# Value and column sums of a segment's attention in 32-row tiles of the PE array, with one half divided before its value sums

## The chip, the cores and the metric

One core of a Trainium2 chip runs the whole program. The metric is device time in microseconds for one execution. Engines are named as in the profile: PE (matmul), PEld (PE's weight loads), DVE (VectorE), ACT (ScalarE), POOL (GpSimd) and SP (which issues most DMAs).

## The reference, cut to what matters

Four blocks follow each other on a sequence of 2048 rows of 512: attention with a recurrent memory, a gMLP mixer, and both again. The attention works through 64 segments of 32 tokens. Each segment sees 8 memory rows ahead of its tokens, and the first 8 rows of its output are the next segment's memory, so that the segments form a chain.

```python
for s in range(n_seg):                                   # 64, one after the other
    h = jnp.concatenate([mem, xs], axis=1)               # 8 + 32 rows
    q, k, v = (einsum('btd,dhe->bhte', h, W) for W in (Wq, Wk, Wv))   # 32 heads of 128
    scores = jnp.where(mask, einsum('bhqe,bhke->bhqk', q, k) * scale, -1e9)
    o = einsum('bhqk,bhke->bhqe', softmax(scores), v)
    o = einsum('bhte,hed->btd', o, Wo)
    mem = o[:, :8, :]; outs.append(o[:, 8:, :])
```

## The kernel before

`a_block` holds one attention block, `b_block` one gMLP block. Inside `a_block`, `segment` is called 64 times. The order of the work on PE, DVE and ACT is the order in which the code records it (`manual_schedule`), and each of these engines takes its instructions strictly in that order. A recorded instruction that must wait holds up all behind it on its engine.

A segment has 40 positions: 8 memory rows, 24 tokens, and 8 last tokens whose rows do not depend on the memory of this segment as keys and are prepared a block of 128 rows ahead. `hT` holds the transposed input rows. `mm_chunk` (L710) projects 32 rows against 512 columns of weights: 16 matmuls in four column groups of 32 (tile 128*32), four K steps of 128. `qk` does so for Q (j = 0, 1) and K (j = 2, 3), each j being half r of the 32 heads; ACT casts the result to `rows`, and DVE turns 32x32 blocks (`qk_T`, L922) into `QQ` and `KA`. `v_mm` makes the values, cast into `VA`. `scores(r)` makes the scores of 16 heads; keys of the last 8 positions come from `KX`, and their values from `VX`. `exps` is ACT's exponential and `close` DVE's product with the mask.

In `close`, `maskN` writes E twice, with alternate groups of 32 rows set to zero, so that `sums_memory`, `pv` and `sums_tokens` (L971, L988, L991, L980) can work with 64-row tiles of the array (64*128 in the profile): two tiles at once, each summing over 64 rows of which 32 are zero. The column sums are divided by afterwards: Ln and Exp on ACT give the reciprocals `Rm` (memory positions) and `Rt` (all others), and DVE multiplies (`memory_out` L1007, `tok_out` L1010, `last_out` L1013). Each half r has its own psO tile of two PSUM banks (`attO0`, `attO1`); psQ and psS share the two-bank tile `att`.

`wo_pairs` (px) and `wo_rest` (pw) multiply the memory rows by Wo. `fold` adds the parts of px (`cross`, `t1`), and `build_hA` adds pw (`memT`, L893) and turns the sum into the next segment's `hT` (L894), which the next Q matmul needs. That is the recurrence.

Between these steps `fill()` takes one step of a generator: `b_units` projects the last 8 positions of the next 128 rows (psb), six chunks in three of every four segments (the fourth has no filler in the first four block rows); `y_part` multiplies finished rows by Wo (pwB). `copies`, `turns` and `adds` collect the casts and additions that follow, and `run` records them. `spare1`, `spare2`, `spare3` place statistics of rows (`x_stats`, `y_stats`) and additions (`y_half`) on DVE; `x_stats` and `y_stats` also append to `copies` a pair of ACT instructions that makes a reciprocal standard deviation (`_rstd_act`, RS in the profile) out of DVE's aggregate (MV).

## Time and profile before

| | |
|---|---|
| Median of 3 runs | 1644.34 us (1640.43 to 1645.09) |
| Span of the profiled execution | 1643.0 us |
| First Q matmul of the first segment | 30.4 us |
| Last Q of the first attention block's 64 segments starts | 687.6 us |
| First Q of the second attention block | 846.1 us |
| A segment, first Q matmul to first Q matmul | mostly 10.157 us; the very first 23.5 us |
| Granted TensorE clock, mean | 0.996 |

The profiled execution's own time is known by its span; the median of the runs is 1.3 us above it. The two gMLP blocks take what is between the attention blocks and at the end, some 145 us each. A line of the timeline gives start, duration, engine, source line, operation, what is written and read, the shape, and how many equal ones follow each other. A matmul's duration includes its drain through the array, which overlaps the matmuls after it; in `128*32` the first number is the tile's rows and the second its columns.

### The profile page before, as it was taken

The numbers are of one execution on the slowest core, as the hardware profiler recorded it, in microseconds if no ns is written. First come the engines' busy times: TensorE is split into PE (matmuls) and PEld (weight loads), VectorE is DVE, ScalarE is ACT, GpSimd is POOL, SyncE is SP. The second block draws the span as 40 slices with busy tenths as digits, with TensorE's granted clock in tenths as the row PEclk, the third lists the DMA queues.
The fourth block names the chain that finished last, engine by engine and source line by source line (L and its number), as shares of the span: only waits on it lengthen the run. The fifth ranks groups of instructions, "written<-read, shape, count | busy, mean of one in ns | idle before, by whom it ended". The sixth has DMA issues, their size and how long they took to land.

```text
span 1643.0 us, 87201 instructions
## 1 busy us (share of the span) xinstructions
PE 1593.0 (97%) x39134; PEld 945.6 (58%) x39134; DVE 1181.5 (72%) x2923; ACT 1072.8 (65%) x2281; POOL 288.1 (18%) x604
## 2 busy tenths in 40 slices
PE   5799999999999999999999999999999999999999
PEld 2455555555656566566655555556566565565565
DVE  3677777778877887884367777777788778878722
ACT  2677777777777777661047777777777777776400
POOL 5111111112211122320011111111122112214000
PEclk9999999999999999999999999999999999999999
DMA  9322121212321333277951222212233224335696
GB/s 362 86 42 42 42 45 42 43 43 75 80 55 43 77 86 80 87 190 143 210 167 46 47 46 46 48 44 45 59 89 86 46 58 95 89 71 155 152 198 159
DMA packets 263598, 148.78 MB, mean 91 GB/s; under 512 B 197560, under 2 KB 239648, under 8 KB 263224
## 3 DMA queue, kind: packets, MB, share of 16 engines
q1 hardware_dynamic: 249992, 99.38, 27.7%
q0 software_dynamic: 13232, 43.82, 8.3%
q8 instruction: 307, 5.03, 1.3%
q14 instruction: 67, 0.55, 0.1%
HBM read 59.68 MB, written 37.19 MB: 59 GB/s over the span
## 4 chain that ended last, share of the span: by engine, by line
PE 55%; DVE 1%; ACT 0%; issue 0%; DMA 0%; SPq 0%; DVEq 0%
PE pg L393 9%; PE psQ L710 7%; PE psK L710 7%; PE psb L710 5%; PE pz L292 5%; PE px L790 4%; PE psm L710 3%; PE psV L710 3%; PE psO L797 3%; PE py L436 2%; PE pwB L809 2%; PE psO L971 1%; PE psO L988 1%; PE psT L980 1%; PE psS L945 1%; PE pw L1237 0%
## 5 line engine op out<-in xcount | busy, mean ns | idle before, releaser
L710 PEld LDWEIGHTS <-hT 128*32 128x32 bf16 x12288 | 332.4, 97 | 309.0 <-DVE hT L894 28.5
L922 DVE STREAM_TRANSPOSE QQ<-rows 128x512 bf16<-128x512 bf16 x256 | 177.7, 694 | 57.6 <-ACT rows L919 57.0
L922 DVE STREAM_TRANSPOSE KA<-rows 128x512 bf16<-128x512 bf16 x256 | 176.1, 688 | 11.5 <-ACT rows L919 6.0
L1010 DVE TENSOR_TENSOR uT<-psO,Rt 128x384 bf16<-128x384 f32 x256 | 140.7, 550 | 36.1 <-ACT Rt L1078 35.7
L919 ACT CAST rows<-psQ 128x512 bf16<-128x512 f32 x256 | 142.4, 594 | 26.2 <-PE psQ L710 23.2
L393 PE MATMUL pg<-z,wspT 128*128 128x344 bf16 x1024 | 154.3, 309 | 0.0
L1078 ACT ACTIVATE Rt<-Rt 128x512 f32<-128x512 f32 x256 | 147.3, 622 | 4.1
L710 PE MATMUL psQ<-Wq_sb,hT 128*32 128x512 bf16 x2048 | 135.1, 382 | 13.1 <-DVE hT L894 9.0
L954 ACT ACTIVATE S<-psS 128x224 bf16<-128x224 f32 x256 | 91.4, 357 | 81.9 <-PE psS L949 81.9
L1007 DVE TENSOR_TENSOR uT<-psO,Rm 128x128 bf16<-128x128 f32 x256 | 74.6, 292 | 96.8 <-ACT Rm L1006 95.8
L880 POOL COPY KX<-old 128x128 bf16<-128x128 bf16 x128 | 69.4, 542 | 384.9 <-PE psS L949 244.5
L790 PEld LDWEIGHTS <-uT 128*32 128x32 bf16 x4608 | 110.8, 96 | 44.5 <-DVE uT L1007 32.2
L710 PE MATMUL psQ<-Wk_sb,hT 128*32 128x512 bf16 x2048 | 135.7, 383 | 0.0
L710 PE MATMUL psm<-Wq_sb,hT 128*32 128x512 bf16 x2048 | 135.0, 381 | 0.0
L790 PE MATMUL px<-Wo,uT 128*32 128x256 bf16 x3840 | 134.8, 274 | 0.0
L710 PE MATMUL psK<-Wk_sb,hT 128*32 128x512 bf16 x2048 | 133.9, 379 | 0.0
L710 PE MATMUL psK<-Wv_sb,hT 128*32 128x512 bf16 x2048 | 133.9, 379 | 0.0
L710 PE MATMUL psV<-Wv_sb,hT 128*32 128x512 bf16 x2048 | 133.2, 378 | 0.0
L1075 ACT ACTIVATE Rt<-psT 128x1024 f32<-128x1024 f32 x128 | 131.1, 1024 | 3.2
L880 POOL COPY KX<-front 128x128 bf16<-128x128 bf16 x126 | 67.9, 545 | 367.9 <-PE psS L949 247.3
L393 PEld LDWEIGHTS <-wspT 128*128 128x128 bf16 x1024 | 100.2, 98 | 53.2
L797 PE MATMUL psO<-Wo_high,uT 128*32 128x128 bf16 x7168 | 125.9, 219 | 2.5 <-issue 1.9
(195 smaller groups left out, 2864.9 us busy)
## 6 DMA issues: line engine op xcount, KB each, us to landing
o_d<-o_sb SPq DMA_DIRECT2D x126, 64.0 KB
vb_d<-front SPq DMA_DIRECT2D x30, 256.0 KB
VX<-vb_d SPq DMA_DIRECT2D x120, 64.0 KB
ln_x<-xd SPq DMA_DIRECT2D x26, 256.0 KB
y_o<-o_d POOLq DMA_DIRECT2D x22, 256.0 KB, 3.4
xd<-y_o POOLq DMA_DIRECT2D x22, 256.0 KB, 2.9
Wq_sb<-in_A_Wq_dram POOLq DMA_DIRECT2D x8, 512.0 KB, 8.8
Wk_sb<-in_A_Wk_dram POOLq DMA_DIRECT2D x8, 512.0 KB, 10.0
```

Of the source, the lines that this page charges most:

```text
L292: nc.tensor.matmul(pz[:, c0:c1], lhsT=xnT[:, kt, :], rhs=w_in_sb[:, kt, c0:c1], start=(kt == 0), stop=(kt == KT - 1))
L393: nc.tensor.matmul(pg[t][:, k, 0:344], lhsT=wsp[t][:, st, :], rhs=z(st, 344 * k, 344 * k + 344), start=(st == 0), stop=(st == NT - 1))
L710: return [nc.tensor.matmul(ps[32 * cg:32 * cg + 32, :], lhsT=lhs(kt, cg), rhs=rhs(kt, cg), start=(kt == 0), stop=(kt == KT - 1), tile_posi ...
L790: nc.tensor.matmul(px[at:at + 32, 0:256], lhsT=lhs[:, h, :], rhs=wo_rhs(h, slice(k + 2, None, -2) if h % 2 else slice(k, None, 2)), start= ...
L797: nc.tensor.matmul(pw[32 * cg:32 * cg + 32, :], lhsT=lhs[:, h, :], rhs=wo_rhs(h, cg), start=False, stop=(h == H - 1), tile_position=(0, 32 ...
L880: eng.tensor_copy(KX[:, :, r].rearrange("p g (k i) -> p i g k", i=4), bs["KTB"][:, r].rearrange("p (i g) k -> p i g k", i=4)[:, :, :, 8 * ...
L919: return r, mms, nc.scalar.copy(r[:], ps)
L922: nc.vector.transpose(out=QQ[:, j % 2, :, 0:32] if j < 2 else KA[:, j % 2], in_=r[:])
L954: return nc.scalar.activation(out=S[:, r], in_=psS[:, r, 0:224], func=ACT.Exp, scale=scale)
L1010: nc.vector.tensor_tensor(out=hview(uT_nxt[:], r, 0, 24), in0=oview(r, 8, 32), in1=rview(r, 0, 24), op=ALU.mult)
L1075: nc.scalar.activation(out=Rt[:], in_=psT[:], func=ACT.Ln)
L1078: nc.scalar.activation(out=rt, in_=rt, func=ACT.Exp, scale=-1.0)
```

## The change

- E is written once (`mask` in place of `maskN`), as one tile per half. `pv` and the column sums of the second half (`sums_one`) use tiles of 32 rows and 128 columns (32*128), four at a time, into one psO tile of four banks (`attO`) for both halves.
- The column sums of the first half (`sums_own`) are made before its value sums, with a matrix `group` of ones in each group of 32 rows, in tiles of 128*32. ACT makes their reciprocals `Rn`, and DVE divides E[0] by them ahead of `pv(0)`. Its results are then copied out of psO (`memory_zero`, a copy for the tokens on DVE, one for the last positions on ACT). The second half is divided afterwards as before (`memory_one`, `tokens_one`).
- `QQ` and `KA` keep two heads side by side, element by element. The casts write `rows` in that order, and DVE turns pairs of 16-bit elements as one 32-bit element (`bitcast(F32)`).
- The last key chunk (j = 3) is made, cast and turned in two halves, the first as PE's third item of the segment, in a bank of the psP tile (tag `attO`).
- V(0) and V(1) are spread over the scores and sums. Casts of j = 1, of the first half of j = 3 and of VA(0) are on DVE, that of VA(1) on ACT.
- Wo's fold: `memT` and its turn are made in two halves of 64 columns; pw has the tile `att1`.
- The fillers step by single K steps: two before the value sums, two after the sums, four at the end. ACT's order after Wo is: collected copies, copy for oB, Ln of Rt, cross, Exp of Rt.

The diff, cut to its core (lines that go are left out where new ones stand for them):

```diff
+    mask = cp.tile([P, 224], BF16, name="mask")
+    m4 = mask[:].rearrange("p (i c) -> p i c", i=4)
+    nc.vector.tensor_copy(m4[:, :, 0:40], maskf[:, 0:160].rearrange("p (i q) -> p i q", i=4))
+    nc.vector.tensor_copy(m4[:, :, 40:56], own)
+    group = cp.tile([P, 4, 32], BF16, name="group")
+    nc.vector.memset(group[:], 0.0)
+    for g in range(4):
+        nc.vector.memset(group[32 * g:32 * g + 32, g, :], 1.0)
...
+        att = [_Tagged(ps_pool, f"att{r}", 1) for r in range(2)]
+        attO = _Tagged(ps_pool, "attO", 1)
...
+        KAr = [pers.tile([P, 2, 8, 32, 2], BF16, name=f"KA{i}") for i in range(2)]
+        QQr = [pers.tile([P, 2, 8, 40, 2], BF16, name=f"QQ{i}") for i in range(NKQ)]
...
+                ps = (accB if early and k % 2 and not alone and not (now and j == 5) else accA).tile([P, 512], F32, name="psb")[:]
+                for kt in range(KT):
                     mm_chunk(ps, lambda kt, cg: bs["hB"][:, kt, :],
-                             lambda kt, cg: qk_rhs(w, j, kt, cg) if j < 4 and now else cols_rhs(w, j, kt, cg), kts)
-                    if kts[-1] != KT - 1:
+                             lambda kt, cg: qk_rhs(w, j, kt, cg) if j < 4 and now else cols_rhs(w, j, kt, cg), (kt,))
+                    if kt < KT - 1 and not early:
...
+                copies.append(out)
+                yield
...
+                                     start=(h == lo and h == WO_PAIR), stop=(h == H - 1), tile_position=(0, 32 * cg), skip_group_check=True)
...
+            eng.tensor_copy(QQ[:].rearrange("p r n q two -> p (r n) two q")[:, :, :, 32:40],
+                            bs["QTB"].rearrange("p r (n two) k -> p (r n) two k", two=2)[:, :, :, 8 * j4:8 * j4 + 8])
...
+            for k in range(2):
+                cols = slice(64 * k, 64 * k + 64)
+                nc.vector.tensor_tensor(out=t[:, cols], in0=pw[:, cols], in1=t1[:, cols], op=ALU.add)
+                nc.vector.transpose(out=rows.hT[s // 4][:, 2 * k:2 * k + 2, at:at + 32], in_=t[:, cols])
...
+            S = [segp.tile([P, 224], BF16, name=f"S{r}", bufs=1) for r in range(2)]
+            E = [segp.tile([P, 224], BF16, name=f"E{r}", bufs=1) for r in range(2)]
+            begin = first and s == 0
...
+            def qk_copy(eng, r, ps, h=0, n=1):
+                return eng(part(r, h, n).rearrange("p (n el two) -> p n two el", el=32, two=2), ps.rearrange("p (n two el) -> p n two el", el=32, two=2))
+
+            def qk_T(j, r, h=0, n=1):
+                t = QQ[:, j % 2, :, 0:32] if j < 2 else KA[:, j % 2, 8 * h // n:8 * (h + 1) // n]
+                nc.vector.transpose(out=t.bitcast(F32).rearrange("p n q one -> p n (q one)"), in_=part(r, h, n).bitcast(F32))
...
+                        nc.tensor.matmul(pS[32 * g:32 * g + 32, 56 * i:56 * i + 40], lhsT=KA[:, r, n // 2, :, n % 2], rhs=QQ[:, r, n // 2, :, n % 2],
+                                         start=(i == 0), stop=True, tile_position=(0, 32 * g), skip_group_check=True)
...
+                nc.scalar.activation(out=S[r][:], in_=psS[r][:, 0:224], func=ACT.Exp, scale=scale)
...
+            def sums_own(pN):
 
                 for k in range(2):
+                    for g in range(4):
+                        o, e = quad(pN[32 * g:32 * g + 32, :]), E[0][:]
+                        nc.tensor.matmul(two_ends(o) if k else o, lhsT=group[:, g, :],
+                                         rhs=e_own(e).rearrange("p i (b e) -> p i b e", b=2) if k else e_all(e, 0, 40),
+                                         start=False, stop=True, tile_position=(0, 32 * g), skip_group_check=True)
+
+            def sums_one(lo, at, n):
 
                 for k in range(2):
+                    for g in range(4):
+                        e = E[1][32 * g:32 * g + 32, :]
+                        o = quad(psO[:, g, at:at + 4 * n])
+                        b = 40 if lo == 0 else 48
+                        nc.tensor.matmul(o[:, :, n - 8:n] if k else o, lhsT=ones[32 * g:32 * g + 32, :],
+                                         rhs=e_all(e, b, b + 8) if k else e_all(e, lo, lo + n), start=False, stop=True,
+                                         tile_position=(32 * g, 0), skip_group_check=True)
...
+                        nc.tensor.matmul(psO[:, g, 160 * r + 40 * i:160 * r + 40 * i + 40], lhsT=VA[32 * g:32 * g + 32, r, i, :],
+                                         rhs=E[r][32 * g:32 * g + 32, 56 * i:56 * i + 40], start=(r == 0 and i == 0), stop=True,
+                                         tile_position=(32 * g, 0), skip_group_check=True)
+                for g in range(4):
+                    nc.tensor.matmul(two_ends(quad(psO[:, g, 160 * r:160 * r + 160])), lhsT=VX[32 * g:32 * g + 32, j4, r, :],
+                                     rhs=e_own(E[r][32 * g:32 * g + 32, :]).rearrange("p i (b e) -> p i b e", b=2), start=False, stop=True,
+                                     tile_position=(32 * g, 0), skip_group_check=True)
...
+            def memory_zero():
+                nc.vector.tensor_copy(hview(uT_cur[:], 0, 24, 32), oview(0, 0, 8))
+
+            def memory_one():
+                nc.vector.tensor_tensor(out=hview(uT_cur[:], 1, 24, 32), in0=oview(1, 0, 8), in1=Rm[:].rearrange("p g (i q) -> p g i q", q=8), op=ALU.mult)
...
+            psQ = att[0].tile([P, 512], F32, name="psQ")
+            qk(0, psQ)
+            psK = att[1].tile([P, 512], F32, name="psK")
+            qk(2, psK)
...
+            qk_copy(nc.scalar.copy, r0, psQ[:])
+            psP = attO.tile([P, 4, 512], F32, name="psP")
+            qk(3, psP[:, 0, 0:256], h=0, n=2)
             qk_T(0, r0)
+            r2 = new_rows()
+            qk_copy(nc.scalar.copy, r2, psK[:])
+            psM = accB.tile([P, 512], F32, name="psm")
+            qk(1, psM)
+            r3 = new_rows()
+            low = qk_copy(nc.vector.tensor_copy, r3, psP[:, 0, 0:256], 0, 2)
             qk_T(2, r2)
...
+            def values(kts):
+                mms = v_mm(0, psP[:, 1, :], kts)
+                other_bank(mms, [low] + high)
+                seen_v.extend(mms)
+
+            def last_keys():
+                mms = qk(3, psP[:, 2, 0:256], h=1, n=2)
+                other_bank(mms, [low])
+
...
+            values((0,))
+            psS[0] = att[0].tile([P, 512], F32, name="psS")
+            scores(0)
+            r1 = new_rows()
+            qk_copy(nc.vector.tensor_copy, r1, psM[:])
+            if not begin:
+                last_keys()
+            exps(0)
+            values((1,))
+            qk_T(3, r3, 0, 2)
+            close(0)
+            values((2,))
+            high.append(qk_copy(nc.scalar.copy, r3, psP[:, 2, 0:256], 1, 2))
+            other_bank(high, seen_v)
             qk_T(1, r1)
...
+            v_mm(1, psW, (0,))
+            pN = psS[0][:, 256:416]
+            sums_own(pN)
+            qk_T(3, r3, 1, 2)
+            values((3,))
+            v_mm(1, psW, (1,))
+            Rn = segp.tile([P, 160], F32, name="Rn", bufs=1)
+            nc.scalar.activation(out=Rn[:], in_=pN, func=ACT.Ln)
+            psS[1] = att[1].tile([P, 512], F32, name="psS1")
+            scores(1)
+            nc.vector.tensor_copy(VA[:, 0].rearrange("p i e -> p (i e)"), psP[:, 1, :])
+            v_mm(1, psW, (2, 3))
+            nc.scalar.activation(out=Rn[:], in_=Rn[:], func=ACT.Exp, scale=-1.0)
             exps(1)
...
+            e = E[0][:]
+            nc.vector.tensor_tensor(out=e_all(e, 0, 40), in0=e_all(e, 0, 40), in1=quad(Rn[:]), op=ALU.mult)
+            own = e_own(e).rearrange("p i (b e) -> p i b e", b=2)
+            nc.vector.tensor_tensor(out=own, in0=own, in1=two_ends(quad(Rn[:])), op=ALU.mult)
+            nc.scalar.copy(VA[:, 1].rearrange("p i e -> p (i e)"), psW[:])
             close(1)
...
+            spare1(E)
+            if not begin:
+                fill(2)
+
+            psO = attO.tile([P, 4, 512], F32, name="psO")
             pv(0)
...
+            sums_one(0, 320, 8)
             pv(1)
...
+            sums_one(8, 352, 32)
+            if not begin:
+                fill(2)
+            memory_zero()
+            Rm = segp.tile([P, 4, 32], F32, name="Rm", bufs=1)
+            nc.scalar.activation(out=Rm[:], in_=psO[:, :, 320:352], func=ACT.Ln)
+            nc.scalar.activation(out=Rm[:], in_=Rm[:], func=ACT.Exp, scale=-1.0)
+            memory_one()
...
             px = accB.tile([P, 512], F32, name="px")
             wo_pairs(px, uT_cur)
...
+            pw = att[1].tile([P, 512], F32, name="pw")[:, 0:128]
...
+            run(copies)
+            nc.scalar.copy(oB_cur[0], oview(0, 32, 40))
+            Rt = segp.tile([P, 4, 128], F32, name="Rt", tag="Rt", bufs=1)
+            nc.scalar.activation(out=Rt[:], in_=psO[:, :, 352:480], func=ACT.Ln)
+            run(turns)
+            spare2()
             cross = wk.tile([P, P], F32, name="cross", bufs=1)
             beside = nc.scalar.copy(cross[0:64, :], px[64:128, 128:256])
+            nc.scalar.activation(out=Rt[:], in_=Rt[:], func=ACT.Exp, scale=-1.0)
             t1 = wk.tile([P, P], F32, name="t1", bufs=1)
             fold(px, cross, t1, beside)
             if s + 1 < NSEG:
                 build_hA(s + 1, pw, t1)
             if s > 0:
                 store_o(s, pw, t1)
+            nc.vector.tensor_copy(hview(uT_nxt[:], 0, 0, 24), oview(0, 8, 32))
             spare3()
+            fill(4)
             run(copies)
+            tokens_one(hview(uT_nxt[:], 1, 0, 24), 8, 32)
+            tokens_one(oB_cur[1], 32, 40)
             run(adds)
```

## The prediction

> **What bounds the kernel now.** I read the page first, then the timeline of one segment of the recurrence, then the busy time of a segment with and one without filler work.

> ```profile
> span 1643.0 us, 87201 instructions
> PE 1593.0 (97%) x39134; PEld 945.6 (58%) x39134; DVE 1181.5 (72%) x2923; ACT 1072.8 (65%) x2281; POOL 288.1 (18%) x604
> ```

> PE looks full. The timeline (start, duration, engine, line) says how full: in a row of n equal matmuls only the last one's drain is idle.

> ```profile
> 303.56 0.39 PE L710 MATMUL psb<-Wq_sb,hB 128*32 128x512 bf16 x4
> 303.88 0.23 PE L971 MATMUL psO<-E,ones 64*128 64x64 bf16 x4
> 303.94 0.31 PE L988 MATMUL psO<-E,VA 64*128 64x80 bf16 x8
> 304.08 0.22 PE L991 MATMUL psO<-E,VX 64*128 64x128 bf16 x2
> 304.24 0.61 PE L710 MATMUL psb<-Wq_sb,hB 128*32 128x512 bf16 x8
> ...
> 305.05 0.43 PE L980 MATMUL psT<-E,ones 64*128 64x512 bf16 x4
> ...
> 305.42 1.05 PE L790 MATMUL px<-Wo,uT 128*32 128x256 bf16 x30
> ...
> 307.41 1.03 PE L710 MATMUL psb<-Wk_sb,hB 128*32 128x512 bf16 x16
> 307.42 0.29 DVE L893 TENSOR_TENSOR memT<-psO,t 128x128 bf16<-128x128 f32 x1
> 307.75 0.31 DVE L894 STREAM_TRANSPOSE hT<-memT 128x128 bf16<-128x128 bf16 x1
> ...
> 308.27 0.39 PE L710 MATMUL psQ<-Wq_sb,hT 128*32 128x512 bf16 x4
> ```

> Nearly every segment takes 10.157 us from its first Q matmul to the next segment's (such as the one at 308.27). PE alone explains it. A projection of 16 matmuls of 512 columns streams for 0.865, a filler round of four 0.215. Per segment: six projections 5.19, two score groups 0.26, 32 filler matmuls 1.72, px 0.99, pw 0.78, and the two stretches with 64-row tiles: from 303.78 (the round of 303.56 has streamed) to 304.24, 0.46, and from 304.68 to 305.42, 0.74. Sum 10.14. Inside those stretches about 0.10 is lost at each change between 128*32 and 64*128 tiles: 303.78 to 303.88 going in; 304.08 plus 0.055 of streaming to 304.24 coming out.

> ```profile
> 104.80:115.00 10.20, 10.20 (x297) 5.81 (x292) 7.52 (x21) 8.22 (x20) 0.47 (x1) 1.00 0.29 36
> 115.00:125.00 10.00, 8.64 (x266) 5.25 (x259) 7.64 (x19) 7.75 (x18) 2.24 (x5) 1.00 0.25 51
> ```

> Columns: length, then busy time of PE, PEld, DVE, ACT, POOL. The second window is a segment without filler: PE is idle 1.4 us, yet the segment takes as long. So the recurrence (new hT, projections, scores, sums, Wo, fold, hT) is itself about 10.0 us. Two limits lie 0.15 us apart, and a change must move both.

> **The change, PE's sum.** Value and column sums for E[1] and the value sums of E[0] become 32-row tiles, four at a time. No row shows that tile; the nearest are the scores, rounds of four 40-column matmuls: 16 take 0.11 of streaming, 25 to 28 ns a round. I take that. pv(r): four rounds plus one of 64 columns, 0.13; sums for the memory two rounds, 0.05; for the tokens 0.08. One stretch instead of two: 0.10 + 0.13 + 0.05 + 0.13 + 0.08 + 0.10 = 0.59 instead of 1.20. Column sums of E[0] against `group` (128*32, 160 and 64 columns) add 0.10; the halved key chunk 0.01. The scores now read QQ and KA at every second element, which no row shows: between nothing (40 columns stream in 17 ns, and the round takes 25) and two cycles an element, 33 ns and 53 for the last round, 0.06 a group, 15 us in all; I take nothing and keep the other end for the range. PE: 10.14 - 0.61 + 0.11 = 9.64. If PE stayed the bound: 126 x 0.51 = 64 us less.

> **The recurrence.** Durations: DVE and ACT rows give a fixed part and about 1 ns (DVE) or 0.83 ns (ACT) per element: DVE 691 for 512 elements from PSUM, 550 for 384, 282 for 128; ACT 594, 357 (224), 277 (128). So DVE's new 256-element cast is 0.42, ACT's 0.38, Ln and Exp of Rn 0.30 and 0.33, a half of memT or hT 0.22, `close` 0.27 (half of 390, with its fixed part). Handing over: 0.22 from the last matmul's streaming end to a reader (0.165 of drain, 0.379 busy less 0.215, and 0.05: px ends at 306.59, `cross` starts at 306.64), 0.03 from ACT to DVE, 0.05 from DVE to PE (hT ends 308.06, its load starts 308.11), 0.07 more where DVE waits on two engines (gaps of 0.10 and 0.03 in the timeline); neighbours on one engine overlap by 0.08 to 0.10.
> The paired turns move 256 four-byte elements where 512 two-byte ones took 694. Between 128 elements (312) and 512 (694) the rows rise 1 ns an element; four-byte elements are in no row. Bounds 0.42 (time by elements) and 0.69 (by bytes); I take 0.42, since the rows' slope is one element a cycle. [...]

> A plain segment with filler, t = 0 at its first Q matmul. Q to 0.86, K to 1.73. The third item, half a key chunk, writes the psO tile, and waits until DVE has done the last segment's tail: second half of hT, o_sb, the uT copy, two token products (0.22, 0.25, 0.55, 0.55, 0.28 less overlaps) end 1.71. Just in time. Then ACT's casts of Q (1.08 to 1.67) and K (1.94 to 2.53), DVE's turn of Q, cast of the half chunk (2.41 to 2.83), turn of K to 3.17; scores(0) start 3.27, when PE is there. Exp, close: E[0] at 4.45; column sums at 4.48; Ln, Exp, two divisions (0.31, 0.21) end 6.05; PE is there at 6.1 after V(1) and two filler rounds. E[1] at 6.42, 0.07 late. The stretch ends 6.75, fillers to 7.28. Here come two new waits. Rm's Ln stands behind `memory_zero` on DVE (6.97 + 0.29), because both read psO: Ln, Exp, product end 8.23, and px's heads from 16 on wait 0.1. And on ACT, `cross` now stands behind the filler cast, the oB copy and Rt's Ln (7.80, 8.30, 8.47 + 0.59): 8.96 instead of 8.61. So t1 ends 9.55, first half of memT 9.66 to 9.88, its turn to 10.0 or 10.1, though pw streamed until 9.17. The four closing filler rounds end at 10.03 and cover it but for the rest: 10.07, PE idle 0.4. The same working for the segment without filler of before gives 9.85, where seven measured 9.91 to 10.14, median 9.99. Half of that shortfall on top: 10.14. A plain segment gains nothing: 126 x -0.02 = -2 us.

> **The segments with statistics lose.** `run(copies)` puts the rstd pair (Ln, Exp, 293 and 203) at the head of ACT's queue, before the filler cast and the cast of Q. It waits for DVE's aggregate, which now stands behind the uT copy: o_sb from 0.26, uT copy to 1.03, BN statistics 413 to 1.36, aggregate to 1.60. In the kernel before, ACT is still in the second Exp of Rt when the aggregate ends, and segments with statistics take 10.157 like the others; now ACT idles for it. Rstd ends 2.15, filler cast 2.65, Q's cast 3.15 instead of 1.67, K's 3.64; turns and cast of the half chunk chain to 4.28; scores(0) at 4.33 instead of 3.27: +1.06. Block rows 0 to 13 of the first attention block have one each: 14 x 1.06 = 15 us. The row sums' segments (`ys`, four groups of seven) have the aggregate alone or an addition (413) before the token products: 0.2 to 0.6 by the same steps, 3.4 a group: 13 us. An addition of pwB (0.69) ahead of Q's turn: 0.19 x 22 = 4. Last and first segments: 3. Sum +35. The gMLP blocks are untouched. POOL's copies and SP's turns of rowsB keep a segment of cover; if that went, some 1 us per block row.

> The profiled execution spans 1643.0, 1.3 under the median of the runs shown, 1644.34, so the sum is put on that: 1644 - 2 + 35 = **1678**.

> **Rivals.** *PE stays the bound.* If the hand-overs are shorter than I sum, in first place `cross` on ACT, so that a plain segment falls under 9.85, the kernel is faster: at 9.75, and with the rstd waits half hidden, 126 x -0.4 + 17 = -33: 1611. For it: 0.4 idle PE time is made of pieces of 0.1. Against it: the no-filler segments ran longer than my sum, not shorter. 0.12. *Even.* Plain segments at 9.88, statistics as computed: -35 + 35, 1644. 0.08.
> *The weight loads bound the 32-row tiles.* The stretch has 56 loads instead of 32. In the trace of before eight loads of 128 columns fit in 0.2 us of PEld, of which the last one's 0.10: 15 ns each if in series. 56 x 15 = 0.84 instead of 0.39, on the path: 126 x 0.35 to 0.45 more, about 1725. For it: four loads per round in place of two. Against it: loads of two row tiles start 3 ns apart. 0.12. [...]
> *Turns by bytes.* 0.27 more for each full turn, two on the path before scores(0) and one later: 126 x 0.7 = +88, 1766. 0.05.
> My own case: 0.63.

> **How the numbers follow.** This kernel's measurement tells 0.3%, 5 us, from no change. Faster 0.12 (first rival), same 0.08 (second), slower 0.80 (the rest). My own case by itself: 1655 (plain 10.0) to 1700 (stretch 0.1 to 0.2 longer than the score rows say). The range takes in the even case and the upper tiles' bound in part: 1636 to 1716.

> **What would show it.** Right: PE idle before psQ (hT) and before scores(0); first-block segments j4 = 2 near 11.1 us; PE's busy share down; ACT's RS waiting on DVE's MV; a stretch of 0.6 with rounds near 25 ns. Wrong: segments under 9.9 us everywhere, or rounds of 50 ns in the stretch, or turns of 0.69.

## The result, and the profile after

The changed kernel takes 1729.62 us (median of 4 runs, 1728.27 to 1732.93) against 1644.01 us: ratio 1.053, 95% interval 1.0513 to 1.0547, 85.6 us more. The forecast had the sign, with 1678 and a range up to 1716, and missed the size by 52 us. The profiled execution spans 1727.8 us, 1.8 under the median. First the page: span, busy times, PE's instruction queue (transfers, MB).

```profile
span 1727.8 us, 99755 instructions
...
PE 1617.9 (94%) x45255; PEld 966.3 (56%) x45278; DVE 1211.0 (70%) x3689; ACT 940.4 (54%) x2153; POOL 282.3 (16%) x604
...
q8 instruction: 354, 5.80, 1.4%
```

PE is busy 25 us longer, at a lower share; it has 6144 more pairs of weight load and matmul, and its instructions came in 354 transfers (307 before). Then the timeline of PE in a segment with filler, the answer to the one shown of before:

```profile
1262.57 0.60 PE L714 MATMUL psb<-Wq_sb,hB 128*32 128x512 bf16 x8
1263.11 0.27 PE L996 MATMUL psO<-E,VA 32*128 32x40 bf16 x16
1263.22 0.19 PE L1000 MATMUL psO<-E,VX 32*128 32x64 bf16 x4
1263.32 0.22 PE L988 MATMUL psO<-E,ones 32*128 32x32 bf16 x8
1263.43 0.27 PE L996 MATMUL psO<-E,VA 32*128 32x40 bf16 x16
1263.55 0.19 PE L1000 MATMUL psO<-E,VX 32*128 32x64 bf16 x4
1263.58 0.24 PE L988 MATMUL psO<-E,ones 32*128 32x128 bf16 x8
1263.74 0.61 PE L714 MATMUL psb<-Wq_sb,hB 128*32 128x512 bf16 x8
...
1265.33 0.95 PE L797 MATMUL pw<-Wo_high,uT 128*32 128x128 bf16 x56
1266.11 1.04 PE L714 MATMUL psb<-Wk_sb,hB 128*32 128x512 bf16 x16
1267.24 0.40 PE L714 MATMUL psQ<-Wq_sb,hT 128*32 128x512 bf16 x4
```

Eight filler matmuls stream 0.43, so the stretch runs from 1263.00 to 1263.74: 0.74 us where two stretches took 1.20. The closing fillers have streamed at 1266.97, and Q waits until 1267.24: PE is no longer the bound. The windows of a segment without filler and of this one (columns as before):

```profile
1057.29:1067.79 10.50, 8.63 (x309) 5.42 (x310) 8.10 (x26) 6.52 (x15) 2.51 (x6) 1.00 0.20 38
1257.00:1267.24 10.24, 10.14 (x340) 6.05 (x340) 8.08 (x27) 6.90 (x16) 0.48 (x1) 1.00 0.42 88
```

Without filler 10.50 (10.00 before), with filler 10.24, one of the shortest; before, 10.157 was the rule. Means over block rows 2 to 14, by j4 and between the starts of the first Q matmuls: 10.76, 10.85, 11.61, 10.99 in the first attention block, 10.78, 10.71, 10.40, 11.02 in the second, against 10.18 to 10.25 in every class before. The mean difference of 0.67 times 126 is the whole loss; from the first Q of the first block's last segment to that of the second block 158.7 us pass (158.5 before). Groups that wait follow (busy, mean ns | idle time ahead, what ended it): first three of them before the change, then the same ones and a division in the changed kernel:

```profile
L797 PEld LDWEIGHTS <-uT 128*32 128x32 bf16 x7168 | 114.0, 97 | 5.4 <-issue 4.7
...
L888 DVE TENSOR_TENSOR t<-px,cross 128x128 f32<-128x128 f32 x128 | 37.3, 291 | 17.1 <-ACT cross L1073 3.5 <-DVE cross L886 0.5
...
L113 ACT ACTIVATE RS<-MV,eps_t 128x1 f32<-128x1 f32 x56 | 16.4, 293 | 94.4 <-DVE MV L137 87.9 <-DVE MV L145 6.5
```

```profile
L797 PEld LDWEIGHTS <-uT 128*32 128x32 bf16 x7168 | 114.8, 97 | 18.0 <-issue 17.2
...
L1087 DVE TENSOR_TENSOR E<-E,Rn 128x160 bf16<-128x160 bf16 x128 | 54.0, 422 | 0.0
...
L889 DVE TENSOR_TENSOR t<-px,cross 128x128 f32<-128x128 f32 x128 | 37.4, 292 | 60.5 <-ACT cross L1126 60.5
...
L117 ACT ACTIVATE RS<-MV,eps_t 128x1 f32<-128x1 f32 x56 | 16.5, 295 | 155.0 <-DVE MV L141 87.4 <-DVE MV L149 67.6
```

Four suspects: the rstd pair waits 67.6 us for the aggregate at L149 (6.5 before); t1 waits 60.5 us for `cross` (3.5 before); the divisions take 0.42 where 0.31 was assumed; and PE idles 17.2 us at pw (4.7 before) while the profile shows nothing that it waits for.

### The profile page after: what moved, and what is told of

Its sections match the earlier page's. It is cut to its first block, busy times and chain, and to the rows that moved or that the text cites. A ratio compares the mean times of both kernels' runs of the same rounds, so it can differ in the third digit from the quotient of the medians.

```text
span 1727.8 us, 99755 instructions
## 1 busy us (share of the span) xinstructions
PE 1617.9 (94%) x45255; PEld 966.3 (56%) x45278; DVE 1211.0 (70%) x3689; ACT 940.4 (54%) x2153; POOL 282.3 (16%) x604
## 5 line engine op out<-in xcount | busy, mean ns | idle before, releaser
L714 PE MATMUL psP<-Wv_sb,hT 128*32 128x512 bf16 x2048 | 179.2, 379 | 0.0
L714 PE MATMUL psV<-Wv_sb,hT 128*32 128x512 bf16 x2048 | 172.5, 379 | 1.6 <-DVE rows L930 1.6
L714 PE MATMUL psP<-Wk_sb,hT 128*32 128x256 bf16 x4096 | 159.2, 274 | 4.5 <-DVE front L1017 2.3
L790 PEld LDWEIGHTS <-uT 128*32 128x32 bf16 x4608 | 111.4, 96 | 77.5 <-DVE uT L1011 50.7
L934 DVE STREAM_TRANSPOSE QQ<-rows 128x256 f32<-128x256 f32 x256 | 112.3, 439 | 52.9 <-ACT rows L930 52.9
L930 ACT CAST rows<-psQ 128x512 bf16<-128x512 f32 x128 | 96.8, 756 | 93.8 <-PE psQ L714 93.7
L797 PE MATMUL pw<-Wo_high,uT 128*32 128x128 bf16 x7168 | 129.0, 219 | 12.5 <-issue 12.3
L790 PE MATMUL px<-Wo,uT 128*32 128x256 bf16 x3840 | 134.7, 274 | 5.1 <-DVE uT L1011 5.1
L934 DVE STREAM_TRANSPOSE KA<-rows 128x128 f32<-128x128 f32 (+1 forms) x384 | 127.6, 332 | 0.0
L797 PEld LDWEIGHTS <-uT 128*32 128x32 bf16 x7168 | 114.8, 97 | 18.0 <-issue 17.2
L959 PEld LDWEIGHTS <-KA 128*32 128x32 bf16 x4096 | 56.9, 95 | 97.8 <-DVE KA L934 69.9
L714 PEld LDWEIGHTS <-hB 128*32 128x32 bf16 x2976 | 71.0, 97 | 64.9 <-issue 23.6
```

Source lines behind the costliest of these rows:

```text
L714: return [nc.tensor.matmul(ps[32 * cg:32 * cg + 32, :], lhsT=lhs(kt, cg), rhs=rhs(kt, cg), start=(kt == 0), stop=(kt == KT - 1), tile_posi ...
L790: nc.tensor.matmul(px[at:at + 32, 0:256], lhsT=lhs[:, h, :], rhs=wo_rhs(h, slice(k + 2, None, -2) if h % 2 else slice(k, None, 2)), start= ...
L797: nc.tensor.matmul(pw[32 * cg:32 * cg + 32, :], lhsT=lhs[:, h, :], rhs=wo_rhs(h, cg), start=(h == lo and h == WO_PAIR), stop=(h == H - 1), ...
L930: return eng(part(r, h, n).rearrange("p (n el two) -> p n two el", el=32, two=2), ps.rearrange("p (n two el) -> p n two el", el=32, two=2))
L934: nc.vector.transpose(out=t.bitcast(F32).rearrange("p n q one -> p n (q one)"), in_=part(r, h, n).bitcast(F32))
L959: nc.tensor.matmul(pS[32 * g:32 * g + 32, 56 * i:56 * i + 40], lhsT=KA[:, r, n // 2, :, n % 2], rhs=QQ[:, r, n // 2, :, n % 2], start=(i = ...
```

## The experiments

Theory A: the named waits make the loss. Theory C: PE's instructions come late. Theory D: the longer casts do it. The edits are made to the changed kernel unless the text says otherwise, and what a run gains is counted from its 1729.62 us; "before" ran with each group at 1642.6 to 1644.9 us.

**Statistics earlier (e1_stats).**

```diff
 def spare2():
+    if first and j4 == 1 and tb + 2 < NB:
+        x_stats(tb + 2, 1)
+        x_stats(tb + 2, 2)     # and y_stats(y, 2); both leave spare3 (code cut)
```

> Edit: the second half of the BN statistics and their aggregate (x and y rows) move from behind the uT copy to DVE's idle slot ahead of `cross`, so that the rstd pair finds its input ready. Theory A, the wait of the rstd pair at the head of ACT's queue costs the segments with statistics: ACT's idle time ahead of RS (67.6 us, 38 times, in the changed kernel) falls under 10; first-block segments j4=2 go from about 11.7 to 10.5 us (14 x 1.2 = 17) and those with `ys` from about 11.4 to 10.7 (28 x 0.6 = 17): about 1730 - 33 = 1697. Rival, these segments are late for PE (instructions that come late) or for the additions on DVE: the idle time ahead of RS goes, and the time stays within 8 us, 1722 to 1730.

Measured 1701.54, ratio 1.0351 (1.0325 to 1.0377): 28 us less. Its group of RS:

```profile
L117 ACT ACTIVATE RS<-MV,eps_t 128x1 f32<-128x1 f32 x56 | 16.1, 288 | 95.6 <-DVE MV L141 87.5 <-DVE MV L149 8.1
```

The wait at L149 is gone, and the j4 = 2 segments of the first block fall from 11.61 to 10.44. Theory A holds for this part.

**`cross` first on ACT (e3_cross), both (e6_both), `cross` behind the filler cast (f1_cross2).**

```diff
 # e3: ahead of run(copies); f1: here; the same two lines leave their place behind spare2()
+cross = wk.tile([P, P], F32, name="cross", bufs=1)
+beside = nc.scalar.copy(cross[0:64, :], px[64:128, 128:256])
 nc.scalar.copy(oB_cur[0], oview(0, 32, 40))
 Rt = segp.tile([P, 4, 128], F32, name="Rt", tag="Rt", bufs=1)
 nc.scalar.activation(out=Rt[:], in_=psO[:, :, 352:480], func=ACT.Ln)
```

> Edit: ACT copies `cross` first, ahead of the filler cast, the oB copy and Rt's Ln. Theory A, `cross` is on the path to hT: DVE's idle time ahead of t1 (60.5 us, 128 of them) goes to about 10, and memT then waits for pw: some 0.2 a segment in the plain ones, 126 x 0.12 to 0.2 = 15 to 25, about 1710. Rival, pw or the fillers behind it end later anyway: idle time moves from t1 to memT, 1725 to 1732; the casts that now stand behind `cross` make tokens late: slower than 1735.

> Edit: both earlier edits together, the statistics in DVE's slot ahead of `cross` and ACT's copy of `cross` ahead of the filler cast. Theory A, two separate waits: the gains add, 1730 - 28 - 20 = 1682. Rival, the statistics now stand where the earlier `cross` has taken the slack (BN and aggregate 0.62 us ahead of the fold on DVE), so that segments with statistics lose again: 1690 to 1700.

> Edit: as the earlier `cross` edit, but ACT's order is filler cast, `cross`, oB copy, Ln of Rt. There the filler cast stood behind `cross`, and the closing filler rounds, which write the same PSUM buffer that this cast reads, started 0.38 us late (9.48 instead of 9.10 us after the segment's first Q matmul). Theory A, the segments with filler gain what that edit gave back: they go to about 10.2 us, and those without filler keep the 0.35 us that they gained: 1695 to 1702. Rival, PE's late instructions decide at pw in the filler segments: no better than the earlier edit, 1708 to 1712.

e3 takes 1710.12, which is 20 us less. e6 takes 1696.98, only 5 better than e1 alone, and this is the rival's number. One cause stands in e3's timeline of PE, behind pw:

```profile
1250.45 1.05 PE L714 MATMUL psb<-Wk_sb,hB 128*32 128x512 bf16 x16 [0.20 <-ACT rowsB L775]
```

The closing fillers write the PSUM buffer that the filler cast reads, and this cast now stood behind `cross`. Besides, the two edits shorten in part the same wait: that of the rstd pair for L149 falls from 67.6 to 27.8 us in e3 too. And the j4 = 2 segments of the first block take 10.69 in e6 against 10.44 in e1, as the rival had it; the runs do not tell these parts from each other. f1 puts the cast first again: 1703.21, ratio 1.0354 (1.0329 to 1.0380), 26 us less than the changed kernel. The plain segments of the second block (median of j4 = 1 and 2, block rows 2 to 13) take 10.18 instead of 10.42, `cross` is done at 9.02 instead of 9.43, and t1 waits no longer than before the change (17.5 and 17.1 us):

```profile
L889 DVE TENSOR_TENSOR t<-px,cross 128x128 f32<-128x128 f32 x128 | 37.3, 291 | 17.5 <-ACT cross L1121 3.5 <-DVE cross L887 0.5 <-ACT old L1122 0.5
```

**POOL's copies away from the divisions (e4_pool, e7_pool).** e4 added a small POOL copy that waits for uT ahead of `prep_segment`; e7 wrote with it into QQ and KX, so that the real copies must follow it.

```diff
 if s + 1 < NSEG:
+    for t in (QQr[(s + 1) % NKQ][:, 0, 0, 32:33, 0], KXr[(s + 1) % NKQ][:, 0, 0, 0:1]):
+        nc.gpsimd.tensor_copy(t, uT_cur[:, H - 1, 24:25])
     prep_segment(s + 1)
```

> Edit: POOL's three copies of a segment (QQ, KX) wait for the last column of uT, so that they run beside the fold and no longer beside the divisions of E[0]. Theory A, POOL and DVE slow each other: the divisions go from means of 0.42 and 0.30 us to 0.32 and 0.22 and E[0] is 0.18 earlier; half of the segments have pv(0) wait for it: 64 to 128 x 0.18 = 12 to 23 us less, about 1713. Rival, the durations belong to the operands (f32 against bf16): they stay, 1728 to 1732. Other operations that POOL now runs beside may grow instead (the turns of memT, the uT copy): then 1730 or more.

> Edit: POOL first writes one element of the QQ and KX buffers from the last column of uT, so that its copies for the next segment cannot start before memory_one (the edit before it had only added an instruction, and the copies still ran beside the divisions). Theory A, the copies slow the divisions of E[0]: these go from 0.42 and 0.30 us to 0.32 and 0.22, and the segments in which pv(0) waits for them gain 0.18: 12 to 23 us, about 1712. Rival, the time goes elsewhere: the copies now run beside the turns of memT, the uT copy and the token product and lengthen those, 1728 to 1735.

e4 missed its aim (1733): the copies still ran where they had run, beside the divisions. e7 moved them:

```profile
L1087 DVE TENSOR_TENSOR E<-E,Rn 128x160 bf16<-128x160 bf16 x128 | 41.8, 327 | 0.0
...
L1089 DVE TENSOR_TENSOR E<-E,Rn 128x64 bf16<-128x64 bf16 x128 | 30.5, 238 | 0.0
```

So POOL was what lengthened them (422 and 297 ns). The time is 1728.18, no change and not the 1712 of Theory A: px starts 0.12 earlier in the plain segments, pw ends 0.11 later, and PE's issue idle at pw rises from 17.2 to 24.7 us. The turns of memT, which the rival had grow, stay at 245 ns.

**Casts that write in order (e2_walk).**

```diff
-ps.rearrange("p (n two el) -> p n two el", el=32, two=2)    # output likewise, "p (n el two) -> p n two el"
+ps.rearrange("p (n two el) -> p n el two", el=32, two=2)    # output likewise, "p (n el two) -> p n el two"
```

> Edit: the casts of Q and K walk their elements in the order in which the pairs are written (output contiguous, PSUM read at a stride of 32 elements), same result. Theory D, the longer casts (ACT 756 instead of 594 ns, DVE 745 instead of 691) come from 2-byte writes at every second element: they fall back to about 0.60 and 0.69. If they are on the path to scores(0), 2 x 0.16 x 126 = 40 us less, 1690; if PE gets to scores(0) no earlier anyway, 5 to 10 less, 1722. Rival, the reading of PSUM out of order costs as much or more: the casts stay at 0.75 or grow, 1728 or more.

```profile
L930 DVE CAST rows<-psm 128x512 bf16<-128x512 f32 x128 | 87.2, 682 | 7.3 <-PE psm L714 0.5
L930 ACT CAST rows<-psK 128x512 bf16<-128x512 f32 x128 | 75.5, 590 | 29.3 <-PE psK L714 29.2
```

The cost was the 2-byte write at every second element: without it ACT takes 590 instead of 755 ns and DVE 682 instead of 745, and reading PSUM at a stride costs nothing (594 and 691 in the kernel before). The time stays at 1728.26. Theory D falls: in the plain segments scores(0) start 3.25 us after the first Q matmul in both kernels.

**Fewer or more PE instructions (e5_fill, f2_fewer, e8_split).**

```diff
 # e5: filler, one instead of four
+nc.tensor.matmul(ps, lhsT=ones[:], rhs=cols_rhs(w, j, kt, kt), start=(kt == 0), stop=(kt == KT - 1))
 # f2: sums_one once with 40 columns (8 matmuls for 16), and
-WO_PAIR = 18
+WO_PAIR = 22
 # e8, in the kernel before: pw in halves
+nc.tensor.matmul(pw[32 * cg:32 * cg + 32, 64 * k:64 * k + 64], lhsT=lhs[:, h, :], rhs=wo_rhs(h, cg)[:, 2 * k:2 * k + 2, :], ...)
```

> Edit: each filler round of four 32-column matmuls becomes one 128-column matmul against a constant weight of ones, 512 columns as before: the projections of the block rows are left out, PE streams as long, and has 48 instructions fewer a segment of some 707. Theory C, PE runs out of instructions after the dense stretches (an idle time of 0.5 to 1.3 us each third segment at pw, each some 1.8 us behind the start of a 16 KB instruction transfer; 37 us in all against 8 in the kernel before): the idle time put down to issue at pw and the value sums falls to under 12 us, the instruction queue's packets from 354 to about 307, and the time by 15 to 28: about 1708. Rival, the idle time is a semaphore that the profile does not show (a transfer, a cast): it stays, 1725 to 1732.

> Edit of the changed kernel: the column sums of E[1] for memory and tokens are made by 8 matmuls instead of 16 (40 columns a head group at once), and WO_PAIR goes from 18 to 22, which makes 84 Wo matmuls of 92, pw 40 of 56, with the same columns streamed; 32 instructions fewer a segment, same result. Theory C, instructions come late in the dense stretch: packets from 354 to about 338, issue idle at pw from 17 us to 12 or less, 8 to 15 us less, 1718. Rival, px ends 0.2 us later and with it `cross` and t1, which are on the path: 1735 to 1755.

> The kernel before, with each 128-column matmul of pw made in two halves of 64 columns: 112 instead of 56 a segment, the same columns streamed, some 14300 instructions more. Theory C, PE's instructions come too late when more of them stand in the same time: the instruction queue's packets go from 307 to about 363, the idle time put down to issue around pw from 5 us to 20 or more, and the time to 1660 to 1680. Rival, only the rounds count: 28 rounds of 27 ns in place of 14 of 54, nothing or up to 5 us, 1643 to 1648; and no idle time of issue.

e5 takes 1723.85, which is 6 us less and not the 15 to 28 expected. Only segments that project block rows lose 48 instructions, 33 on average (338 transfers, not the 307 expected). f2 takes 1716.87, 13 us less, although px is longer. e8 takes 1783.47, ratio 1.0842 (1.0816 to 1.0867), far above the 1660 to 1680 expected: 139 us more for an edit that streams the same columns. A pw without a stall streamed for 0.94 instead of 0.78, some 20 us in all, and the rest is PE waiting for nothing:

```profile
PEld L710 <- issue: 76.1, 99, 2.9
PEld L798 <- issue: 67.4, 72, 2.3
```

(The waits of e8, in us, times, longest. At L710 some of it is the start of the program, as in the kernel before: 27.1.) Where these stalls stand can be read from the trace's records. Counted in program order, 47 of the 48 stretches of over 0.2 us (from 60 us on) in which the changed kernel's PE neither streams nor loads, and that the profile puts down to issue, end with number 194 modulo 256, at whatever line that is: pw, a value sum, a filler. In e8 it is 113 of 114. A packet of the instruction queue has 16384 bytes, and there is one packet for 256 PE instructions: PE's records are 78616 before, 90705 in the changed kernel (with one matmul for each weight load) and 92952 in e8, 307, 354 and 363 times 256 and a rest, which are the numbers of transfers. From the trace of the changed kernel, us (a few boundaries around 1270):

```
boundary passed   next transfer starts   took    next boundary passed   idle before it
1242.01           1242.86                1.11    1245.57                0.77
1253.52           1254.45                1.07    1257.67                none
1269.88           1273.04                0.97    1275.37                0.98
1275.37           1276.44                1.42    1279.39                1.29
```

A stall mostly ends 1.3 to 1.6 us behind the end of a transfer (median 1.42), in every kernel looked at. Where PE stalls, a boundary follows the one before by a median of 3.6 us: 1.0 to the start of the transfer, 1.05 for it, 1.4 until PE goes on.

**Five edits together (f3_all), with fewer Wo matmuls (f4_all22).**

> All the edits that have shown a wait: statistics ahead of `cross`, `cross` ahead of the oB copy and Rt's Ln, POOL's copies held until memory_one, casts that write without a stride, and the column sums of E[1] in 8 matmuls. Theory A, the waits add up once none of them is hidden behind another: statistics 28, `cross` 30, divisions 10, sums 5 to 10: about 1660. Rival C, PE's late instructions (about 30 us) now decide where the waits did, and take half of it: 1675 to 1690.

> The edit before it, with WO_PAIR 22 as well. Theory C: fewer instructions in pw, 5 to 10 us less than without, and the issue idle at pw under 10 us. Rival: px ends 0.2 us later, `cross` and t1 with it, and pw's end is no longer the last: 5 to 12 us more than without.

f3 takes 1653.75, ratio 1.0053 (1.0035 to 1.0070), 76 us less than the changed kernel and still slower than before. f4 takes 1660.96, 7 us more than f3, as the rival forecast: its px lasts 0.23 us longer. In f3, PE fills nearly all of the first segment below and all of the last, which is shorter than the 10.157 of before:

```profile
982.21:992.48 10.27, 10.15 (x337) 6.19 (x337) 7.67 (x26) 6.94 (x17) 1.60 (x5) 1.00 0.26 73
...
952.34:962.29 9.95, 9.95 (x336) 6.17 (x336) 7.36 (x24) 6.64 (x17) 1.13 (x4) 1.00 0.19 39
```

The means are still 10.16 to 10.39, and 35 us of idle time at the boundaries are left.

**Where the boundaries fall (g1_align, g2_shift, g3_after, then g4_free, g5_dense, g6_after).** Weight loads of a constant, whose result is not used, fill each segment to 768 PE instructions.

```diff
+def pad(cg, n=1):
+    for k in range(min(n, left[0])):
+        nc.tensor.ldweights(ones[:, 0:32], tile_position=(0, 32 * ((cg + k) % 4)))
+    left[0] -= min(n, left[0])
```

> All edits of f3_all, and some 104 more weight loads of a constant a segment (13800 in all, their result never used), spread between the matmuls of the projections, so that each segment has 768 PE instructions and the 256-instruction boundaries always fall at the same three places, 3.3 us apart: K's fifth matmul, the column sums of E[0], the middle of px. Theory C, PE stalls where less than about 3 us lie between two boundaries: the idle time at boundaries (35 us in f3_all) falls under 8, and although there are 15 percent more instructions and 54 more transfers the time falls to about 1630. Rival, the number of instructions decides: more idle time, 1665 or more. If the added loads cost PE time (104 x 7 ns a segment), up to 90 us more, without idle time.

> The same added weight loads a segment, but the boundaries fall 136 instructions earlier or 120 later: before the value sums and near pw's end, with the dense stretch of value sums, px and pw between two of them (about 2.9 us). Theory C: a stall of 0.2 to 0.6 us in each filler segment, idle time at boundaries 20 to 50 us, 20 to 45 us more than with the boundaries at the other places. Rival: the same time as g1_align within 5 us.

> The changed kernel itself with added weight loads (11800) that put the boundaries at K's fifth matmul, the column sums of E[0] and px's ninth matmul. Theory C: its 38 us of idle time at boundaries fall under 10, and the time by 20 to 30, to about 1703; what is then left of the loss against 1644 are the statistics, `cross` and the divisions. Rival: 1730 or more.

They take 1896.09, 1898.64 and 1879.63. With the added loads PE's rounds took longer, most of all in the half chunks: a round of four 256-column matmuls took 0.222 instead of 0.107 us. With segments that long the idle time at the boundaries fell to 1.7, 7.2 and 2.8 us, and nothing could be read from the time. The second three put the loads only at 512-column matmuls:

> All edits of f3_all, and 103 more weight loads a segment of a constant whose result is not used, at most one ahead of each matmul of 512 columns (in segments without filler the rest stands where the filler would be), so that each segment has 768 PE instructions and the 256-instruction boundaries always fall at the ninth matmul of K's half chunk, the end of scores(1) and the start of pw, at least 3.1 us apart. Theory C: the idle time at boundaries (35 us in f3_all) falls under 8 and the time from 1654 to about 1630, below the kernel before, with 15 percent more instructions. Rival, the time hangs on something else and the idle time moves: 1650 or more.

> The same loads, with the boundaries 62 instructions later, at the start of the value sums and inside pw, about 2.6 us apart. Theory C: a stall of 0.2 to 0.6 us at pw in nearly each filler segment, idle time at boundaries 20 to 50 us, and 20 to 45 us more than g4_free. Rival: the same time as g4_free within 5 us.

> The changed kernel with added loads in the same manner (boundaries at the same three places), and no other edit. Theory C: its 38 us of idle time at boundaries fall under 10 and the time by 15 to 30, to about 1705. Rival: 1725 or more, since the waits for the statistics, `cross` and the divisions stand where the stalls stood.

They take 1796.55, 1795.25 and 1817.82. My expectation was wrong: where the boundaries fall does not decide. The idle time at them is 103 us both in g4 and in g5, only at other lines, and it grew in g6 as well, to 69. Against f3, g4 loses 143 us, of which this idle time makes 68; whether the loads cost PE time here too is not told apart. g4's waits:

```profile
PEld L743 <- issue: 58.6, 116, 2.9
PEld L994 <- issue: 50.0, 95, 2.2
```

L994 is the end of scores(1), in no dense stretch; boundaries planned 3.1 us apart or more still stalled, since one follows another only after a median of 3.9 us here. So the instruction supply has a rate, not only a latency. Together (instructions in a segment with filler; gaps of 0.15 us or more between PE's weight loads at a boundary, a weight load being what PE issues ahead of each matmul, 39134 of each in the kernel before):

```
kernel     per segment   transfers   stalls   idle us   time us
before     588           307         26       7.8       1644
f2_fewer   650           338         41       17.9      1717
f3_all     666           346         74       34.8      1654
after      682           354         61       37.6      1730
e8_split   700           363         134      128       1783
g4_free    768           400         224      103       1797
```

At 3.6 to 3.9 us for 256, an estimate from the rows above, 588 instructions can be had in 8.3 to 9.0 us, 682 in 9.6 to 10.4 and 768 in 10.8 to 11.7. The estimate bounds a segment from below and does not give its time: e8's 700 can be had in 9.8 to 10.7 by it, and its segments take 11.2 to 11.5. The change brought this third limit from well under a segment's time to just beside it.

## Why the prediction was right or wrong

**The stretch: mechanism right, 0.15 short.** Rounds are as taken: sixteen 40-column matmuls are busy 0.27 like sixteen of the scores. The scores themselves, which now read every second element, stream 0.11 as before (sixteen matmuls from 303.42 to 303.53, and from 1260.26 to 1260.37 in the changed kernel), so nothing of the 15 us kept for the range was paid. I forecast 0.59 and it is 0.74; the sum left out gaps between the groups inside the stretch (VX at 1263.22 streams some 0.03, the sums start at 1263.32). What makes these gaps is not shown.

**Turns right, casts wrong, neither decides.** A paired turn of 256 elements takes 439 ns (0.42 forecast), what the line through the two-byte turns of before gives for 256 (312 for 128, 694 for 512): elements count here, and not bytes, with about 1 ns more for each element along that line, the slope that the forecast calls one element a cycle and that the rows show in ns alone. The casts were taken at 594 and are 755, a term mis-sized, and e2 shows that it costs nothing.

**The statistics right.** Forecast 15 for j4 = 2 and 13 for `ys`, 28 together; e1 took 28 us away by moving just this work.

**"A plain segment gains nothing: -2 us" failed.** That is the step. Such a segment was forecast at 10.14; the plain segments of the second block have a median of 10.42, and if the other terms held, as the statistics did, nearly all of the 52 us by which the forecast fell short are here. (Its own sum, 1644 - 2 + 35, gives 1677, not 1678.) Two things were in it. The first is the fold: `cross` was to start at 8.96, t1 to end at 9.55, and the turn of the first half of hT, which Q waits for, to end at 10.0 or 10.1, covered by the closing fillers "but for the rest". The medians are 9.16, 9.75 and 10.36, and PE waits; f1's 26 us are the price of `cross` standing late in ACT's queue. The divisions, taken at 0.31 and 0.21, are 0.42 and 0.30, but e7, where they are 0.33 and 0.24, is no faster. Why POOL's copies beside them lengthen the divisions is not shown.

**A term was missing altogether: PE's instructions.** This is the second thing. I counted matmul rounds and weight loads, and put the supply of instructions at nothing without a reason. Idle time at boundaries went from 7.8 to 37.6 us. The kernel before already showed 4.7 us of "issue" at pw, and I did not ask what it was. The period of these stalls, 256 instructions, was read from the changed kernel's trace only afterwards (47 of 48).

**Do the parts add up?** 28 us (e1) and 26 us (f1) are each shown by removal, but no run has just these two edits. They may overlap: f1 alone already lowers the rstd pair's wait for L149 from 67.6 to 43.5 us, and e1 and e3 together gave 33 us of 48. If they add, 31 us remain. The growth of the boundary idle time, 30 us, is of that size, but what it costs alone is not shown: f2 took 20 us of it away and gained 13, e5 15 and gained 6, and no kernel removed it without another cost. The five edits of f3 gain 76 us together with 35 us of this idle time still there, although e7's and e2's gained nothing alone; that what one wait freed was taken by the next limit is how I read it, and not shown.

**The rivals.** "The weight loads bound the 32-row tiles" gave 1725, nearly the number, for the wrong reason: the stretch is 0.74 and not 0.84 plus its switches, and e1 and f1 removed 28 and 26 us without touching it. "PE stays the bound" is refuted by PE's waits for hT, and "turns by bytes" by 439 ns.

## What to carry to other kernels

Before a change that splits matmuls, count PE's instructions per period as a resource of its own, beside streaming time; idle time of PE put down to "issue" that recurred each 256 instructions was that resource running out here. When a step moves on one engine, go through everything that queues behind it: the same `cross` copy gained 20 us ahead of the filler cast and 26 behind it. And a term that was mis-sized by 27% (the casts) can be worth nothing, while one with the right size (the statistics) pays in full; only taking it away in a run tells.
